# Three new tables for a fixed program: order, engines of copies, and buffers

## The chip, the core and the metric

One core of a Trainium2 chip runs the whole program. The time is device microseconds of one launch, the median of three runs. The core has five instruction queues that run side by side, each strictly in its own order: TensorE (PE, matrix products and transposes; its weight loads are listed as PEld), VectorE (DVE), ScalarE (ACT), GpSimd (POOL) and SyncE (SP, which only issues DMA transfers here). They wait for one another through semaphores.

## What is computed

Three layers follow each other on a batch of 2, with 768 rows each:

```python
# 1: attention, 8 heads of 64; q and k only meet in the same hash bucket of 6 bits
mask   = q_bucket[:, :, :, None] == k_bucket[:, :, None, :]
attn   = softmax(where(mask, q @ k.T / 8, -1e9))
x      = (attn @ v)                                  # (2, 768, 512)
# 2: four experts, each a causal attention of its own; two experts per row are weighted
for e in range(4):
    a    = softmax(causal(x @ wq[e] @ (x @ wk[e]).T / 8))
    out += gate_e * (a @ (x @ wv[e]) @ wo[e])
# 3: mix each row with the row before it, then a gated two-layer network
xk, xr = mu_k * x + (1 - mu_k) * x_prev, mu_r * x + (1 - mu_r) * x_prev
y      = sigmoid(xr @ w_r) * (relu(xk @ w_k) ** 2 @ w_v)
```

Precision is kept by splitting numbers into a high and a low half of 16 bits. Almost every tile so has a "hi" copy (a conversion) and a "lo" subtraction behind it, and every product is made of three.

## The kernel before

The rows are worked in 12 blocks of 128 (`i` = 0 to 11; blocks 0 to 5 are the first of the batch). For each block there are steps:

- `query_steps(i)`: load q, split it (`naq`), transpose it (`x2`), hash it (`z_q`), mark the buckets (`nbq`), transpose them (`x1`). `key_steps` does the same for the keys (`nak`, `nbk`, `y2`, `y1`) and splits the values.
- `lsh_steps(i)`: for each head `h`, PE makes the scores `s_i_h`; DVE scales them and takes the minimum (`P`); ACT takes the exponential; ACT or POOL makes the hi half of `PHL_i_h`; POOL always makes the lo half (TENSOR_TENSOR); a DMA transposes `PHL` into `PT_i_h`; PE multiplies that with the values into `x_i`. Heads 0 and 3 of the first four blocks are transposed by PE instead (`tp0`, `tp1`). At the end DVE divides (`x32`), PE transposes, and ACT and DVE split (`xT_i`).
- `moe_steps(i)`: `qk_i`, `vg_i` (values and gate), the experts' scores `se`, their softmax (`PHL_m...`), the product `y_i`, the output `o_i`.
- `mix_steps(i)`: `mk_i` and `mr_i`, the hidden layer `h_i`, the gate `r_i` with its sigmoid `e_i`, the last product `v_i`, and the store.

The weights are loaded and split on the way (`w32_...`, `raw_...`, `wd_...` into `WQK`, `WVG`, `WO`, `WK2`, `WR`, `WV2`).

None of this sets the order. `Program.add` only records operations. At the end `Program.arrange` unpacks three packed tables: `ORDER` is a permutation of the 2,498 recorded operations, and its restriction to one engine is that engine's queue; `ENGINES` says for each conversion copy whether ACT, DVE or POOL does it; `HOMES` says in which buffer of its pool each tile lives:

```python
for o, e in zip(self.ops, unpack(engines, np.uint8)):
    if e:
        o.move("PVAG"[e])
self.order = [self.ops[i] for i in unpack(table, np.uint16)]
```

Since `issue` emits everything from one line, every instruction has the line L225; they are told apart by tile names. Each DMA takes one of eight semaphores (`DMAHW0` to `DMAHW7`), in turn and in the order of the table, and is issued only when the transfer that had this semaphore before has landed. So at most eight are under way, and a late one holds the queue that issues its successor.

Of the kernel before, what the change touches and what calls it, by code (L numbers as in the profile page):

```python
# [982 lines left out]
"""

HOMES = """
c-lpjjdI&K5QBkT{!>j`MYVN0yYe|_=l$QXpgKvEnOLI5B^LPBfUcAS=rw|RaJqTcElCd^m<{?i7MKNt(IVT}rA57OgpL2!iSO`C3$z5Ez;DDW>;>B3KY@SAf587}ziB
^!U*!L=qf$X5JOy@Z45ZYQnjN%BN9l7SUhGAu5q~d^JM9f7*+d-Abv;#HeMYr6wZKHz-V98vI-?i1P#N9SSdCpTWEIg_Q|Wm11*4JUYC1AE7CTn1^2F|Mx6L2VB3Dj`s
*7*>m=2GOsgo^}Q?sBl(Hvzmq+SmNn_nCsmpiOSwdplcE{tw&_c!<Z!Z&QlMSEtOIkw1EmR3-w3`vfL=%aZ#oI>W53>U0lz7%3AYO%AC$-T?DlggMsANp>aahHPnlfSU
ohARCHp$6GsS&%p>KxQpYIih${aq0L_uac6{Smj((BNK}x&4Y^aST4BkXI^<``{BD?aH8DTONPLfDtZKZs!pqgBh*1vu`9n0pm6GwO9_G(<uwV7Rg1RIUU=JXJY$wAHr
r-<hHN$uf{*VU@G4N$kmPTblRYYCB#(pBmW3%Uc2FCpv2@rqfM*km8@I2VhH$u&DkefGNJYcr^t?G9cQ3fx^<u01yo_;BsoI0+689mZMkSM5(TEg{hT(dQ)(2k(#)PVz  # L990
bUWCv;`7e6E_U*FU$&jw0|Ls1N6xIQQ%`EiOrcegJj%$tZT-SlM-roRQ&ox7)9JoFvCq2*R$S}JaZ^oJN7Fo5P=xv;`e74FZIm5Y@2h{Rl}}B<D6!05)#0eVsN!vXNc&
B`bM>=VnKA+w94s!+M(`b}YCtH5Bco<P9!e5E=eUk6g_RJL(M?$@a6I&0J!{<d`6;NYzpsm}t13Vf7L<zSQ-M|ysUb|o5BA6Oot95SR9>p}d*Dh!JPAS%36LM+sh)3kw
#?snwLkXh9s2
"""
# [48 lines left out]
```

## Time and profile before

| what | us |
|---|---|
| median of three runs | 458.5 (457.54 to 459.17) |
| the profiled execution, its own time | 459.79 |
| its span, first to last instruction | 458.0 |
| PE busy in it | 417.8 |
| POOL, DVE, ACT busy in it | 354.7, 346.1, 333.1 |
| mean granted share of PE's clock | 0.988 |

The span is what the rows below divide up; 1.8 us of the profiled time lie around it. Busy time of an engine says nothing about whom the others wait for: that is read from stretches of the span and from waits.

### The profile page before, as it was taken

Reading aid. Unit: us, or ns where it says so; the run is one execution under the profiler, and the core shown is the slowest. Engines: PE = TensorE matmul, PEld = TensorE weight load, DVE = VectorE, ACT = ScalarE, POOL = GpSimd, SP = SyncE. Lnnn points to the kernel's source line nnn. Section 1 sums busy time; section 2 is a strip of 40 time slices with the busy share of each in tenths; the row PEclk is TensorE's granted clock in tenths of the full one; section 3 lists DMA queues with packets and bytes.
Section 4 is the critical chain, followed back from the end, with each engine's and each line's share of the span. In section 5 each row is a group of like instructions: output and inputs, shape, how many; then the busy total and the mean of one; then the engine's idle time right before and its main releaser. Section 6 shows DMA issues by size and latency. Waiting matters only on the chain.

```text
span 458.0 us, 15085 instructions
## 1 busy us (share of the span) xinstructions
PE 417.8 (91%) x6080; PEld 318.0 (69%) x6080; DVE 346.1 (76%) x908; ACT 333.1 (73%) x634; POOL 354.7 (77%) x359
## 2 busy tenths in 40 slices
PE   2847777899899999999999999999999999999996
PEld 2725565678776778686668868786668689856772
DVE  2899998999999889899677787875778674635232
ACT  3998989999899797588986647787746658453230
POOL 5899999899998869799998998978878946462010
PEclk9987999999999999999999999999999999999999
DMA  8989999999999998889999999999698793357101
GB/s 215 276 201 204 210 223 212 231 210 204 213 238 187 166 183 152 206 144 149 191 169 197 158 171 154 190 146 155 124 169 118 140 156 68 74 114 176 36 24 46
DMA packets 227157, 75.54 MB, mean 165 GB/s; under 512 B 218512, under 2 KB 222736, under 8 KB 227088
## 3 DMA queue, kind: packets, MB, share of 16 engines
q1 hardware_dynamic: 225584, 74.48, 86.5%
q8 instruction: 47, 0.77, 0.7%
q10 hardware_dynamic: 1504, 0.11, 0.2%
q14 instruction: 22, 0.18, 0.2%
HBM read 22.14 MB, written 3.15 MB: 55 GB/s over the span
## 4 chain that ended last, share of the span: by engine, by line
PE 56%; DMA 12%; POOL 12%; DVE 8%; issue 6%; ACT 5%; ACTq 0%; POOLq 0%; DVEq 0%
PE h L225 12%; PE v L225 10%; DMA PT<-PHL 9%; PE x L225 6%; PE r L225 6%; POOL PHL L225 6%; PE s L225 6%; PE qk L225 4%; PE se L225 3%; PE vg L225 3%; PE o L225 2%; PE y L225 2%; DVE P L225 2%; ACT P L225 2%; DMA pr<-in_proj_dram 1%
## 5 line engine op out<-in xcount | busy, mean ns | idle before, releaser
L225 POOL TENSOR_TENSOR PHL<-P,PHL 128x768 f16<-128x768 f32 x96 | 160.7, 1685 | 14.9 <-ACT PHL L225 12.2
L225 DVE TENSOR_SCALAR_CACHE_REDUCE P<-s 128x768 f32<-128x768 f32 x96 | 90.5, 951 | 13.0 <-PE s L225 4.5
L225 ACT ACTIVATE P<-P,mx 128x768 f32<-128x768 f32 x96 | 89.2, 930 | 14.4 <-DVE P L225 10.4
L225 PE MATMUL s<-y,x 128*128 128x384 f16 x384 | 77.6, 330 | 2.4 <-DVE P L225 1.9
L225 PE MATMUL h<-mk,WK 128*128 128x128 f16 x1152 | 73.0, 219 | 0.6 <-DVE g L225 0.6
L225 PE MATMUL x<-v,PT 128*128 128x64 f16 x1728 | 62.6, 193 | 9.2 <-DMA PT<-PHL 7.6
L225 PEld LDWEIGHTS <-WK 128*128 128x128 f16 x1152 | 67.1, 98 | 5.1 <-issue 1.0
L225 PEld LDWEIGHTS <-PT 128*128 128x128 f16 x1728 | 58.2, 98 | 16.9 <-DMA PT<-PHL 9.6
L225 PE MATMUL v<-WV,k2h 128*128 128x512 f16 x192 | 57.1, 379 | 0.0
L225 PEld LDWEIGHTS <-x 128*128 128x128 f16 x480 | 38.1, 98 | 23.1 <-issue 5.8
L225 ACT ACTIVATE PHL<-P 128x768 f16<-128x768 f32 x53 | 44.1, 839 | 10.4 <-DMA PT<-PHL 3.7
L225 POOL TENSOR_TENSOR PHL_m<-P_m,PHL_m 128x512 f16<-128x512 f32 (+2 forms) x24 | 33.9, 1418 | 10.6 <-ACT PHL_m L225 9.9
L225 POOL TENSOR_SCALAR PHL<-P 128x768 f16<-128x768 f32 x43 | 37.8, 880 | 5.1 <-DMA PT<-PHL 2.0
L225 PE MATMUL qk<-xT,WQK 128*128 128x128 f16 x576 | 37.7, 219 | 0.3 <-POOL WQK L225 0.3
L225 PE MATMUL v<-WV,k2l 128*128 128x512 f16 x96 | 36.4, 379 | 0.0
L225 PE MATMUL r<-WR,mr 128*128 128x512 f16 x144 | 35.7, 379 | 0.0
L225 PEld LDWEIGHTS <-WQK 128*128 128x128 f16 x576 | 33.5, 98 | 2.0 <-POOL WQK L225 0.5
L225 ACT ACT_TABLE_LOAD x20 | 25.7, 1283 | 11.8 <-PE r L225 8.0
L225 ACT ACTIVATE P_m<-P_m,bias_m 128x512 f32<-128x512 f32 (+2 forms) x24 | 19.7, 822 | 14.5 <-DVE P_m L225 13.9
L225 PEld LDWEIGHTS <-k2h 128*128 128x128 f16 x192 | 17.1, 98 | 15.9 <-issue 0.4
L225 POOL TENSOR_TENSOR mk<-m32k,mk 128x512 f16<-128x512 f32 x12 | 14.0, 1164 | 15.7 <-issue 15.4
L225 ACT ACTIVATE t<-h 128x512 f32<-128x512 f32 x24 | 14.2, 593 | 16.0 <-PE h L225 14.8
(168 smaller groups left out, 861.3 us busy)
## 6 DMA issues: line engine op xcount, KB each, us to landing
raw_k<-in_moe_w_k_dram SPq DMA_DIRECT2D x8, 512.0 KB, 5.7
raw_v<-in_moe_w_v_dram SPq DMA_DIRECT2D x8, 512.0 KB, 4.6
k<-in_k_dram SPq DMA_DIRECT2D x8, 384.0 KB, 4.1
q<-in_q_dram SPq DMA_DIRECT2D x12, 256.0 KB, 4.6
v<-in_v_dram SPq DMA_DIRECT2D x8, 384.0 KB, 5.3
out_dram<-e SPq DMA_DIRECT2D x12, 256.0 KB, 2.9
raw_r<-in_moe_w_r_dram SPq DMA_DIRECT2D x4, 512.0 KB, 5.5
PT<-PHL SPq DMA_TRANSPOSE x88, 4.6
```

What stands on the lines that cost most here:

```text
L225: getattr(getattr(self.nc, engine), method)(*[real(a) for a in args], **{k: real(a) for k, a in kw.items()})
```

## The change

The program, its operations and their number stay the same: PE keeps 6,057 matrix instructions and as many weight loads in the built program, SP its 140 transposing DMAs. All three tables are replaced. A line of each stands for the whole:

```diff
 ORDER = """
-c-jrr0|OXT7XZ+E?|T<-wr$(CZQHhO+qP|^=GAQ0P-D%k_I>9^9D-O-6xu;aC<hL*KtvD#C=Uu*p%_$x63_;sL2+mgrC=xwfih45N<&%jkPWIrHDHJU1~Fk6RD|JB8LB
+c-jrr0|OXT7XZ-v?z?)kZQHhO+qP}nwrv|VuV%A`8f#{??>j%@#DYpt6iPxnKxhvU0iX>OgL04s1hRq$h4N4wx<NFk02QGtWCw$6PzFjtTZjOqAv#orT#y5Xz)+|RWuY
...
 HOMES = """
...
 ENGINES = """
-c-pO%*%pH!3`EJy|NnEX#gwp_0C`ZBlksK&Qz{Hes=;rF>&<({dqubMQ}>OZ8lNRv37y_^Sf|!xGCOKwQj+5@kTsxZz^Lk5s1f5Og);L_1R4$mzZu==K==4i<(L&4wi3
+c-pO2ff9uv2#f9i|M^{(sV}DBMO|l#FmO=EaS6`{+Q9DlGIuMK8|AXLh=0v0R%hrdpv~14@NmQ?Z{LXa057s9IF12&Z;wfV8wwMpv9}&Zd-S}qJCTTgjp+k5x_(V(8ap
```

Of the conversion copies 194 change engine: 57 go from ACT to POOL and 57 from POOL to ACT, 42 from ACT to DVE and 38 from DVE to ACT. PE's first product of a hidden layer, the order of blocks and the kinds of work in each stretch stay where they were; within a stretch nearly every row moves. Three places show how.

The first is the start of ACT's queue, up to its first conversions; `pr` is the hash projection (in two halves), `consts` the matrix of ones that PE's transposes use, `ties`, `muk` and `mur` small tables. Before:

```order
L225 DMA pr_72<-in_proj_dram 64x6
L225 DMA muk<-in_moe_mu_k_dram 128x4x1
L225 DMA pr_72<-in_proj_dram 64x6
L225 DMA consts<-in_consts_dram 128x384
L225 ACT_TABLE_LOAD
L225 ACTIVATE nak_1_0_99<-k_0_1_0_76 128x12x64 [waits DMAHW1_49]
L225 ACTIVATE nbk_1_0_80<-k_0_1_0_76 128x12x64
L225 DMA ties<-in_ties_dram 128x16 [waits DMAHW0_49]
L225 DMA mur<-in_moe_mu_r_dram 128x4x1 [waits DMAHW2_49]
```

and the same stretch after:

```order
L225 DMA muk<-in_moe_mu_k_dram 128x4x1
L225 DMA pr_82<-in_proj_dram 64x6
L225 DMA mur<-in_moe_mu_r_dram 128x4x1
L225 DMA consts<-in_consts_dram 128x384
L225 DMA ties<-in_ties_dram 128x16 [waits DMAHW0_49]
L225 ACT_TABLE_LOAD
L225 ACTIVATE nak_1_0_92<-k_0_1_0_76 128x12x64 [waits DMAHW1_49]
L225 DMA pr_82<-in_proj_dram 64x6 [waits DMAHW2_49]
L225 ACTIVATE nak_1_1_105<-k_0_1_1_94 128x12x64 [waits DMAHW3_49]
```

`mur` has moved ahead of `consts`, one half of `pr` has moved behind the first conversion, and `ties`, which waits for the transfer before it on its semaphore (that of `pr` before, of `muk` now), stands ahead of the table load and of the first conversion instead of behind two of them.

The second is POOL's queue where block 3 of the first layer and block 1 of the experts are fed (`PHL_3_7` is head 7 of block 3; `PHL_m1_p0` and `p1` are the pairs of experts of block 1). Before:

```order
L225 TENSOR_TENSOR PHL_3_0_1873<-P_3_0_1673,PHL_3_0_1873 128x768
L225 TENSOR_SCALAR PHL_m1_p1_1917<-P_m1_p1_1781 128x512
L225 TENSOR_SCALAR gt_1_1813<-gt_1_1813 128x16
L225 TENSOR_TENSOR mk_0_1876<-m32k_0_1745,mk_0_1876 128x512
L225 TENSOR_TENSOR PHL_m1_p0_1971<-P_m1_p0_1762,PHL_m1_p0_1971 128x512
L225 TENSOR_TENSOR PHL_m1_p1_1917<-P_m1_p1_1781,PHL_m1_p1_1917 128x512
L225 TENSOR_SCALAR gs_1_1950<-gs_1_1950 128x1
L225 TENSOR_TENSOR PHL_3_6_2004<-P_3_6_1879,PHL_3_6_2004 128x768
L225 TENSOR_TENSOR PHL_3_4_1957<-P_3_4_1618,PHL_3_4_1957 128x768
L225 TENSOR_TENSOR PHL_3_7_2097<-P_3_7_1914,PHL_3_7_2097 128x768
```

and the same stretch after:

```order
L225 TENSOR_TENSOR PHL_3_0_1863<-P_3_0_1723,PHL_3_0_1863 128x768
L225 TENSOR_SCALAR mk_0_1948<-m32k_0_1769 128x512
L225 TENSOR_SCALAR gt_1_1866<-gt_1_1866 128x16
L225 TENSOR_TENSOR mk_0_1948<-m32k_0_1769,mk_0_1948 128x512
L225 TENSOR_TENSOR PHL_3_4_1935<-P_3_4_1606,PHL_3_4_1935 128x768
L225 TENSOR_TENSOR PHL_m1_p1_1987<-P_m1_p1_1742,PHL_m1_p1_1987 128x512
L225 TENSOR_SCALAR nbq_98<-q32_5_543 128x8x64
L225 TENSOR_SCALAR PHL_m1_p0_2093<-P_m1_p0_1870 128x512
L225 TENSOR_SCALAR raw_v23_0_2031<-raw_v23_0_2031 128x512
L225 TENSOR_TENSOR PHL_m1_p0_2093<-P_m1_p0_1870,PHL_m1_p0_2093 128x512
L225 TENSOR_TENSOR PHL_3_7_2037<-P_3_7_1868,PHL_3_7_2037 128x768
```

`PHL_m1_p0` has moved behind `PHL_3_4`, next to `PHL_3_7`, while `PHL_3_4` and `PHL_3_6` (two rows above this piece) stand ahead of the experts; `mk_0` has a POOL conversion that ACT made before, and `PHL_3_0` and `PHL_m1_p1` have lost theirs to ACT.

The third is DVE's queue around the transposed queries of block 6 (`x2_6`, which PE's hash product `z_q6` reads). Before:

```order
L225 TENSOR_TENSOR xT_4_3262<-tr_x_4_3246,xT_4_3262 128x512
L225 TENSOR_SCALAR P_5_7_3290,mx_5_2720<-s_5_7_3150 128x768
L225 TENSOR_SCALAR P_5_2_3297,mx_5_2720<-s_5_2_3264 128x768
L225 SCALAR_TENSOR_TENSOR h_1_0_3215<-h_1_0_3215,t_1_0_3320 128x512
L225 COPY x2_6_3299<-tr_x2_6_3292 128x512
L225 TENSOR_REDUCE vg_3_3163<-gt_3_3282 128x4
L225 TENSOR_TENSOR k2l_1_3348<-h_1_0_3215,k2h_1_3328 128x512
L225 SCALAR_TENSOR_TENSOR g_3_3375,gs_3_3376<-vg_3_3163,ge_3_3342 128x4
L225 SCALAR_TENSOR_TENSOR vn_0_1338<-vg_3_3163,vn_0_1338 128x256
L225 TENSOR_SCALAR P_5_6_3408,mx_5_2720<-s_5_6_3337 128x768
L225 TENSOR_SCALAR y_3_3379<-sme_3_3039,gs_3_3376 128x4
L225 TENSOR_SCALAR lg_4_3414,gm_4_3415<-vg_4_3395 128x4
```

and the same stretch after:

```order
L225 SCALAR_TENSOR_TENSOR m32r_2_3100<-o_2_2980,mur_84,x2t_2_3047 128x128
L225 COPY x2_6_3247<-tr_x2_6_3223 128x512
L225 TENSOR_SCALAR P_5_6_3310,mx_5_2911<-s_5_6_3288 128x768
L225 SCALAR_TENSOR_TENSOR h_1_0_3232<-h_1_0_3232,t_1_0_3308 128x512
L225 TENSOR_TENSOR k2l_1_3368<-h_1_0_3232,k2h_1_3337 128x512
L225 TENSOR_TENSOR z_q6_3339<-z_q6_3339,zl_q6_3365 128x8x6
L225 TENSOR_SCALAR y_3_3312<-sme_3_3027,gs_3_3283 128x4
L225 TENSOR_SCALAR P_5_7_3373,mx_5_2911<-s_5_7_3348 128x768
L225 RECIPROCAL y_3_3312<-y_3_3312 128x4
L225 TENSOR_TENSOR xT_4_3395<-tr_x_4_3376,xT_4_3395 128x512
```

Before, DVE copies one half of `x2_6` and ACT the other. Now DVE copies both (the first one stands seven rows above this piece), and `xT_4` has moved from ahead of `P_5_7` and `k2l_1` to behind them. The two copies of `x1_7`, the transposed bucket marks of block 7 that its scores `s_7` read, go from ACT to DVE as well; the later one stands in row 394 of DVE's queue of instructions, counted from 0, where `e_2` stood before (row 390 was `x32_6`).

## Rows read from the trace of the kernel before

**Rows 1.** The page: span, then busy time, share, instructions by engine.
```profile
span 458.0 us, 15085 instructions
PE 417.8 (91%) x6080; PEld 318.0 (69%) x6080; DVE 346.1 (76%) x908; ACT 333.1 (73%) x634; POOL 354.7 (77%) x359
```

**Rows 2.** Stretches: start:end, length, busy us (instructions) by engine, PEclk, DMA share, GB/s.
```profile
0.00:120.00 120.00, 88.32 (x1326) 68.87 (x1327) 104.78 (x260) 104.74 (x206) 108.67 (x114) 0.96 1.03 218
120.00:440.00 320.00, 315.57 (x4630) 240.40 (x4629) 237.28 (x644) 225.28 (x424) 245.99 (x246) 1.00 0.86 153
20.00:120.00 100.00, 78.28 (x1176) 59.78 (x1175) 94.21 (x237) 92.34 (x188) 95.11 (x94) 0.95 1.04 210
100.00:140.00 40.00, 38.23 (x632) 31.57 (x631) 38.53 (x102) 38.24 (x77) 38.17 (x39) 1.00 1.19 215
0.00:111.30 111.30, 80.93 (x1200) 63.08 (x1201) 96.73 (x241) 97.35 (x191) 100.42 (x107) 0.95 1.01 217
164.00:232.00 68.00, 66.51 (x1058) 51.87 (x1057) 58.47 (x142) 55.38 (x102) 59.31 (x59) 1.00 0.92 170
```

**Rows 3.** Waits of PE to 125 us: on what, total us, times, longest.
```profile
PE tr_y L225 <- DMA consts<-in_consts_dram: 9.0, 1, 9.0
PE x L225 <- DMA PT<-PHL: 6.6, 5, 2.5
PE tr_x L225 <- DVE nbq L225: 5.0, 2, 4.8
```

**Rows 4.** Waits of PE from 125 us on, same columns.
```profile
PE x L225 <- DMA PT<-PHL: 1.1, 1, 1.1
PE z_q L225 <- DVE e L225: 1.0, 1, 1.0
```

**Rows 5.** ACT, first 5 us: start, took, instruction; then landing times by issue; then queues.
```profile
1.32 0.59 ACTq L225 DMA_DIRECT2D muk<-in_moe_mu_k_dram  x1
3.14 1.28 ACT L225 ACT_TABLE_LOAD   x1 [3.14 <-issue]
4.43 0.84 ACT L225 ACTIVATE nak<-k 128x768 f16<-128x768 f32 x1
muk<-in_moe_mu_k_dram ACTq DMA_DIRECT2D x1, 2.0 KB, 5.6
consts<-in_consts_dram ACTq DMA_DIRECT2D x1, 96.0 KB, 6.4
mur<-in_moe_mu_r_dram ACTq DMA_DIRECT2D x1, 2.0 KB, 4.6
q10 hardware_dynamic: 1504, 0.11, 0.2%
```

**Rows 6.** Chain of waits, 90 to 125 us: start, length, what. PE back to back.
```profile
95.41 1.34 PE vg L225 x12
97.47 0.65 PE s L225 x4
```

**Rows 7.** Timeline of PE and POOL around 118 us.
```profile
108.06 3.27 POOL L225 TENSOR_TENSOR PHL<-P,PHL 128x768 f16<-128x768 f32 x2
118.18 0.70 PE L225 MATMUL x<-v,PT 128*128 128x64 f16 x18 [1.31 <-DMA PT<-PHL]
```

**Rows 8.** Groups of one kind: count, busy us, mean ns of one, idle before.
```profile
L225 POOL TENSOR_TENSOR PHL<-P,PHL 128x768 f16<-128x768 f32 x96 | 160.7, 1685 | 14.9 <-ACT PHL L225 12.2
L225 POOL TENSOR_SCALAR raw_v<-raw_v 128x512 f32<-128x512 f32 x8 | 5.3, 671 | 0.1
```

**Rows 9.** Timeline of DVE and PE, near 164 and near 222 to 232 us.
```profile
163.18 0.42 DVE L225 COPY x<-tr_x 128x512 f16<-128x512 f16 x1
164.28 0.35 PE L225 MATMUL z_q<-prhl,x 128*128 128x12 f16 x8
221.65 0.81 PE L225 MATMUL s<-y,x 128*128 128x384 f16 x4
231.52 0.68 DVE L225 TENSOR_TENSOR x<-x,rs 128x512 f32<-128x512 f32 x1
```

More of the change, by code (lines that the diff above doesn't have):

```diff
@@ new lines @@
+7J8QoCpFjmzR%Kpi&_euf=T+}(9Ua4BSURop%I*8S(MxLR%yWb#9C7-shO-3izU@7#0uz@3D;t|OFlKU_b^<{G+FP}^m9%b`CGhT(YC)pN^W1?+<N?lg3Q>RjJ_c7S8y
+g=^$qx<C8~{N1gD(KrS>!$a4=oq<Pg6<l*8v8rqAM&TE?8rQ%Y{NTpHWB1Cvc8t5B3tV@<xyi5x*1}%+%dLiu>hPl*4>w#Bw-5eyO&#JoXy)eNez@swxdYI`t%pVQrx(
+obpSZ8?sZ+cJx7`M~<G#6;&M>Qg=9{}#ZZ3Lk?V{nouB}^(8=;N+<RW1^m&2chowy6Hz&hLn-`zay<t{_OKioeqBKCGyA)6nIeO(_H1+T$4T#xhdJe-3AxEl{*KiA&<0
+)t#9M>y17hw&I47vLi7;0C)J@GDHi$T-YRzzZ<Mb#W6Qi;sXgeSg>04RBF$mh0vw;seO#hr5Z;*)7D5ZaQwli!cRlLJZ99ySqs^1xL8NzK6@>W8y166({2!eBl>kEbQr
@@ new lines @@
+C`+UBD{|#RHf$ky1#;LFu3;N$-3667dF%CY0@$ME(gOM)3pWx!*W_%1AaFkn$%kVaA!O`vsjCEt&L>C{oVj^td@4zHC*(Jb+zL4LKGw?1<f_-=owqZMe9H+R1m>AppL%
+1AQ;48QfGu%}76lUTqJdD%abaw=2x|LYi&vx7KBxc9OZWZRhB-p_x$G;#2&c-<|7jDF#@fddWui+0kg-hI0H_y#?U40Rs9+To+x5)kFi~2@BC3f=}@Nb_Rb7CfJ?koBo
+_{MkgnelH(g+Jk2e-z*O#{Lbwh3CGrZ{aiIJ1FKCxYT$8(_l%z(0%mpeI87PY4J}ujZJ(hU)ry7pZo{^44y+J-`$_VZ*Uetd-xY{4p+P4ex+OC%J`R%7fbjxZV6?<@6g
+o$g86VU{R3;=I#=EQ3%}xemlb>Z%D#$Eht2$dP{Wt?Rs9b*j~DPNg1d;9@w4ye%lRvK3FElJ_y=CYLfFUOz?Qze|KhJ>5iE$=Fh9m~1+b?76Knanu9yGnpJP#s?{4A)y
@@ new lines @@
+oI;%4&KE;%Um(6;QRXoE}{D!ox6t*aVagQ;@HZsphT{kFM-SG8P@hC@tgNl&)4_mv9+(`R}xWM-^RbdGPsKB`qFqGmpi7!R2Em$8d^&c$h%Vb2z&dNSPqlWI@&-RX+1?
+HbV-Ta0MG6>tbpRW_&5}olF?(_;5NEVZnKL=HSj%r_kF#(ia5~M#LD;zh5q&1-4<tVkpIvB<6q-oKg2)5kMI;D(g)b#l#I5zZLSIimz;+BVLm>6f=E;yKSM37gd_cMzt
+in<yWKnd0()F4`r*IA2>%{y;|JX9_PNyb7DxHWwBNnKsBQ<1@nikpSQR6<(LMpCAfUf6qKih++((Q;j$%_Jcfd8W==2G9QbLOCV$c#F#eK%5J|$(Qnf?oY!+$Uht@2+n
+EoGqSE+(a;)gEb<kKwXXOt;3za?AW$Kikjo|6y$R9rw{emx&I!!!8>+t--M<J^hP6a6bjV+^_K7kMl>Ic<}T6M8D2g!(FtS=K4f5-cR<E`~fn*iKh6YZi1icGtwT)LfL
@@ new lines @@
+77U+C-L3EE6`xE43SmA)>cKS_15K01Gjrg_wPe!AaF>aS2etj&vjO>T%+X_MdR8(}@ZO-=DM9ic5$pBrNnoZ%brW`BpyP!4K_&9Mb8_6O+@<)pjR61VtV)STD*4Zaa?(
+uTa%7p5Xql$vq}&PT;)o6ke{XuID^_vtJhrmE7IoA3_bjJMHFpO;EdZtBPdsS{tO^Hhj_qZXW>j?yh^g(c|$6{iB!id%APY=hV6I+dc*bc4vR=Q7lpyYn$>i;t-XZ>L{
+qw{M4g{T{!|x5p0H5r3r`vRRjLCp=C+(a%J>f%p4;zAJa*1O5q>qc+@{kND&M9CgOS{w5vt8~Flt!M41dyCVBT{vutXt=f*e;X^v=SMUk{l&a8AzCBlyZCswZV-M_!Kl
+`e*ovTp=>V@aI3s<L=yoIYvS?bBXxHtFXid2*O@I+qA{dp^&^p$8G*PutVn%8gyzlwjSi2juC%Y%3b*QW;b2i26?GK?Ei9U07<c?UP5ojiqyaxK}#yLk`q<Gs9zhjSz!
@@ new lines @@
+#qa0JbdV46Q9i(teO(#A$G8?v<$+vJYEyk_AmjJ~|4A*Vq1@w(Jc*xCQ+iI5xd~0<I@H*rhPo8hpW()ImM`&f{)K<yU%4f<qG*0PU*>vrm|xR<e!xHT3tGT4IJ&>WNB9
+-Jp@rO>PVfjG$)k8YzoQubBR%9rJd0maOh22OQEQsXSNR;D<Wqc||DqfGmgaCGAIrz~f75R~fj?71|AoHNH+oMA{3n{r^Y{bB_rG%-KcD0J?{t$B`!>{;npis;&GGzV{
++E*YYy2O1e!@xpV{T7N_#aB<8%Yx}CSJ<SO=S#6;amJC-{!#4LUJF0g~xJ4KIZRo3g1}%;FNx{bfP<)LRg#0GoB)kxSyQnj+DxaHkTh1iKhy1RGuc$So!~9vFcFiF9T$
+tMCPE;8TlzcXVWo~+7FWmn#RB24m4I`aAz7WFZmUBk{;59rpq8n>(lvh@;Arizj%f;v#vBkMoMgMAuT0(Nbg%oXXzqwIUe_?p7Mq-`Zh9Hx=KIlOWo-`ccW1fi(AVj-%
@@ new lines @@
+YwpTj@!0xDUPNw|v=O@ewsXC*U6Rk@IOUiKOrN3y+rx(p&n-H~!B5a9>Ht(KWw*;H&<uPsAzp6MyB;JXd09WKGO5wHKZ7QFMsRmZ&;Wj=6vNv~MS=be>F-a~|ZTZ!iC`
+6O{8ln$8k01+;@?*Mj=1|Ha?%g|ws0m!wQ`!C&)RbdChM?o;wMP0lkVwWiS|oK}-@1j(ThC9)*e(Q?ag*GRHMcj->O=QC&$z3(6RC=yjta9q9PQ!z_nz3uOMkp;3_)9^
+xBB&j(g|KNxIH=j|XNgT<kizS!-?jQLqoQWTM6_e-^Pt$8mNyjlHw`S%iJ}t+Rq#9TD=uetSOXvWKrLlFXq~~<HL{>;1&8&O%XN|AT?Tnt#78Xb2NfwPQSv9`2w6mH_T
+iH2HuIKfT7S{yY)Rsw6O{fWEr6iOTx?EaY2ER&9>UB+|H*}3;(>9h!e$mx(Sl7xrDXIH3iR{<MdP<+@dg)EcB&j5pjgnkaN(R{^Mf8GhkO}lux67}3KriYM{X-|x4#_N
@@ L999 @@
-9W4xS^el*<M@AXt{Dcq%YlrD3|;p+_V206KFpK>d;
+c-pO2ff9uv2#f9i|M^{(sV}DBMO|l#FmO=EaS6`{+Q9DlGIuMK8|AXLh=0v0R%hrdpv~14@NmQ?Z{LXa057s9IF12&Z;wfV8wwMpv9}&Zd-S}qJCTTgjp+k5x_(V(8ap
+^ND%*=~%J*K&9Lv<avji5~s{$0f)`p5}BU-3fZNlkmGruWX^!Q`Ul?k7M&X+?xf)hRKKsltOBx=b(vXS8?XQ>*oY{kJjDwkqdW!#eF*#z8qP(7Cmn~VUZ(r2pw#E2>pv
+#W#!|CtOh@@;*`x}w3v_0VQG-Iw9-<E#HU;VQYzbTiQ=cWChg->U(W
 """
```

76 lines of the change are left out of this document (25 added, 51 removed).

## The prediction, made before the changed kernel ran

> **What bounds the kernel now.** I read the page first: TensorE is busy 417.8 of a span of 458.0 us [rows 1], so it is idle for 40.2. The stretches say where: in the first 120 us it is busy 88.3, idle 31.7; from 120 to 440 it is busy 315.6 of 320, idle 4.4 [rows 2]; the last 18 us hold the remaining 4.1, with the last product, sum and store. From 120 us on the kernel is TensorE's own work, and an order can win there only the 4.4. Whatever is to be won is won in the front, or lost anywhere.
>
> The front is bound by all three of the other engines at once: from 20 to 120 us POOL, DVE and ACT are busy 95.1, 94.2 and 92.3 of 100 [rows 2]. TensorE eats ahead of them and then waits. Its waits by releaser, up to 125 us: 9.0 for `consts` at the very start, 6.6 for the transposed `PT` (five waits, the longest 2.5), 5.0 for `nbq` [rows 3]. Behind 125 us only small ones are left: one `PT` of 1.1 and `z_q` for 1.0 [rows 4].
>
> The longest-lasting of these decides: the `x_3` product of head 7, at 118.18, which had waited 1.31 for its DMA, and whose POOL instructions started at 108.06 and ran 3.27 as a pair, so ended at 111.33 [rows 7]. From POOL's end to TensorE's start lie 6.9 us of issue, transfer and landing. Up to 111.3 us POOL had been idle 10.9 [rows 2]. So POOL's queue ahead of `PHL_3_7`, its idle time and the landing time set when TensorE leaves the front.
>
> **The change, part by part.** The totals of each engine stay nearly equal (57 conversions each way between ACT and POOL, 42 against 38 between ACT and DVE), so I cost nothing for the exchanges as such; their cover is that the sums are the same, and without it each POOL conversion costs about 0.7 [rows 8]. I look at where in the queues the rows stand. All sums are on the profiled span of 458.0 and carried to the median, 458.5 (the profiled execution took 459.79, 1.8 around its span).
>
> *Start.* Before, `consts` lets TensorE begin at 9.0 [rows 3]. `muk` was issued at 1.32 and landed 5.6 later, at 6.9; ACT's table load (1.28) and first `nak` (0.84) ran meanwhile, done by 5.3 [rows 5]. Now `muk` is first, a position of 0.6 earlier, and lands at about 6.3; `ties`, which waits for it, stands ahead of the table load. ACT is blocked until 6.3, then issues (0.59), loads (1.28), converts (0.84): 9.0. The low half on DVE comes behind it, about another conversion of 0.8. TensorE's first transposes so start at 9.0 to 9.8; I take +0.8, since the low halves are needed in the same first run of transposes. Behind the blocked ACT stand its next conversions, for which POOL and DVE wait; they have copies of their own that hang on loads, not on ACT. Ends: 0, and +4.6 if `consts`, with `mur` now ahead of it, comes later by the whole landing time of `mur` (4.6) [rows 5].
>
> At this place a rule speaks against the change. The row: the queue that carries these small tables has 1,504 packets for 0.11 MB, and a 2 KB table takes 5.6 to land while the 96 KB of `consts` takes 6.4 [rows 5]. The Trainium skill, page "DMA: Bandwidth & Descriptors", section "Rules for kernel authors", says that a strided last dimension is turned into one descriptor for every element. `muk` and `mur` are loaded in that form, 512 elements each; by that rule the packet count agrees, and `consts` would stand behind 1,024 descriptors, not 512. By the row alone `consts` goes beside the small tables and not behind them (it landed 2.0 behind `muk`), and the sum has +0.8; by the rule it would have more, which is rival D.
>
> *Landings in the front.* For each `PT` I took TensorE's work ahead of its product and POOL's work ahead of its low half, each instruction at its duration; the difference is the room for POOL's idle time and the landing. For head 7 of block 3, the tightest before, TensorE now has a `vg` (1.34), an `s` (0.65) [rows 6] and an `x_3` of another head (0.5 to 0.7 [rows 7]) more ahead, less two transposes of about 0.35 each: +1.8. POOL has 107 rows ahead in place of 109; the difference of two conversions at 0.67 [rows 8] is 1.3, or 0.9 when the exchanged ones are each taken at their own size; I take 0.9. So head 7 gains 2.7. But other heads come next: head 1 of block 3, earlier 1.0 looser than head 7, moved 2.8 earlier in both queues and keeps its room. It is now the tightest, so the front gains 1.0, if POOL idles as long as before. That is what I take: −1.0. Ends: 0, if TensorE merely waits for something else in the front; −2.7, if head 1 comes with a smaller landing time. The gain is bounded by 6.6, all `PT` waits of the front.
>
> *DVE at `z_q6`.* Before, the copy of `x2_6` ends at 163.60 and the product starts at 164.28 [rows 9]: 0.7 to spare. Now DVE copies both halves, with as many instructions ahead, and TensorE has 2.3 us less work ahead of the product (scores of block 5 and one `r_1` moved behind). It would arrive 2.3 earlier and wait 1.6 at that pace; if DVE fills some of its 9.5 us of idle time from 164 on (58.5 busy of 68 [rows 2]) a little earlier, nothing. I take the middle, +0.8. In this place DVE's `m32r` and `P_5` rows are queued behind the copy and ACT's exponentials behind those.
>
> *Late waits.* The `PT` of 1.1 and the `z_q` of 1.0 [rows 4] have 4 and 20 us more room by the same reckoning of work ahead: −2.1. Ends: 0 (others take their place) and −4.4, all idle time from 120 to 440.
>
> *The tail.* The order of the last block's work is kept; 0.
>
> Sum: +0.8 −1.0 +0.8 −2.1 = −1.5, so 457.0. The ends of the terms that are not rivals of their own, put together as they would rarely all fall, give 454 to 459.5.
>
> **Rivals.** A, slower, at one place: DVE comes late to `s_7`. Both copies of `x1_7` are now on DVE, the second in its row 394. Before, DVE was at this point (row 390) at 231.52, while TensorE started the first `s_7` at 221.65 [rows 9]. TensorE now has 4.9 us more work ahead of the score concerned (products of `v_2`, `o_4`, `x_6`), so wants it at 226.5. At the old pace of DVE that is a wait of up to 5.5 once the copy and its semaphore are added: 458.5 + 0.8 + 0.8 + 5.5, less the 3.1 of the other gains, = 462.5. It decides if DVE fills less than half of its 9.5 us of idle time between 164 and 232 [rows 2]. For it: the idle time hangs on TensorE's products, which come no earlier. Against: from 100 to 140 us DVE filled 38.5 of 40 [rows 2], so it can go at 96% when work is there; at that share it would be in time. Chance 0.17.
>
> B, no change: the front is bound by the sum of the three engines' work (95, 94, 92 of 100 [rows 2]), the room is not used, and the waits that vanish are replaced by others of equal length. +0.8 at the start, −0.3 at the rest: 459.0. For it: equal totals; three engines above 92% have little left to move. Chance 0.23.
>
> C, a larger gain: waits of POOL and TensorE feed each other. POOL idles 4.9 us in 20 to 120 [rows 2]; if half of that goes (−2.5) together with the 4.4 of TensorE's idle time behind 120, less 0.5 lost at the start: 452. For it: nearly every landing of the front has 1 to 3 us more room, the later ones 4 to 8. Against: POOL's idle time must be caused by TensorE, and in the front it is also caused by loads. Chance 0.15.
>
> D, `consts` late: the tables of single elements are carried in front of it. It lands 2.0 to 4.6 later in place of the 0.8 (by the distance of `consts` from `muk` and by `mur`'s own landing [rows 5]), which shifts everything: 458.2 to 460.8, about 460. For it: the packets, and that 2 KB take nearly as long as 96 KB; against: `consts` landed only 6.4 after its issue with one such table ahead of it, less than 1 us longer than that table alone. This is what the rule of the Trainium skill's page "DMA: Bandwidth & Descriptors" would make of the start. Chance 0.05.
>
> **How the numbers follow.** The forecast has 0.40. Differences within 0.3% (457.1 to 459.9) are about what a measurement of this kernel cannot tell from no change. The forecast lies at that edge: of its 0.40 I put 0.22 on faster, 0.14 on same, 0.04 on slower. A gives 0.02 same and 0.15 slower; B 0.06, 0.13 and 0.04; C 0.15 faster; D 0.01 same and 0.04 slower. Together 0.43 faster, 0.30 same, 0.27 slower. The range must take in most of C and of A, since cases of both signs hold most of the chance: 451 to 464, with C's 452 and A's 462.5 inside and their own uncertainty of about 1 us. The likeliest case's own range stays 454 to 459.5.
>
> **What would show it.** Start: TensorE's first instruction at 9.0 to 9.8, waiting for `nak` and not for `consts`; if for `consts` at 11 or later, D. Front: TensorE's busy time in the first 120 us at 88 to 90, `PT` waits below 6.6 in sum, the last of them at head 1 of block 3. Then: a wait of `z_q6` for DVE's `x2_6` below 1.6. If `s_7` waits several us for `x1_7` near 226, A. From 120 to 440, 2 to 3 us of idle time are left in place of 4.4; if busy time there stays at 315 to 316, the late waits were replaced and B holds. The prediction is wrong by more than its own range if DVE, and not POOL with its landings, paces TensorE between 120 and 240, or if POOL's idle time in the front moves by more than 2 us either way, for the whole room rests on its staying as it was.

## The result and the profile after

The changed kernel is slower: 464.56 us, median of four runs (463.61 to 464.83), against 458.65 for the kernel before in the same comparison (four runs, 457.54 to 459.17). The ratio is 1.0128, with a 95% interval of 1.0104 to 1.0152. A second comparison gave 463.37 and 1.0101 (1.0069 to 1.0133). In that one and those below, single runs of the kernel before lie between 456 and 462 us, so the intervals below are 0.2 to 0.4% to either side.

The page of the changed kernel: its span, then busy time of the engines (compare [rows 1]).

```profile
span 463.0 us, 15093 instructions
PE 419.9 (91%) x6080; PEld 319.2 (69%) x6080; DVE 353.6 (76%) x912; ACT 330.5 (71%) x628; POOL 351.8 (76%) x359
```

The span is 5.0 longer. DVE is busy 7.5 us more, with four instructions more. That is the first odd thing: four copies like the one in [rows 9], 0.42 us each, would cost 1.7.

The stretches of the changed kernel (start:end, length, busy time by engine from PE and PEld to POOL, clock, DMA share, GB/s):

```profile
0.00:120.00 120.00, 88.32 (x1319) 69.33 (x1320) 106.55 (x257) 104.32 (x206) 106.41 (x113) 0.96 1.03 213
120.00:240.00 120.00, 113.57 (x1730) 87.66 (x1729) 106.63 (x266) 98.51 (x181) 103.44 (x102) 1.00 0.99 178
240.00:440.00 200.00, 199.00 (x2877) 150.93 (x2876) 135.88 (x384) 124.63 (x238) 139.96 (x144) 1.00 0.83 139
```

and the middle one in the kernel before, which its rows above do not show apart:

```profile
120.00:240.00 120.00, 117.45 (x1780) 90.03 (x1779) 105.24 (x268) 102.11 (x191) 107.10 (x104) 1.00 1.01 181
```

In the first 120 us TensorE is busy 88.32 in both kernels [rows 2], so its idle time in the front is the same. The new idle time lies in the middle. From 120 to 240 us TensorE is idle 6.4 us, against 2.6 before, and ACT and POOL are busy 3.6 and 3.7 less, while DVE is busy 1.4 more. Nobody but DVE is busy longer, and everybody else waits.

Idle time is not the whole loss. Over the span it rises by 2.9 us: 3.9 more from 120 to 240 us, 0.9 less from 240 to 440, 0.1 less behind. The other 2.1 of the 5.0 us are busy time, 419.9 against 417.8 for the same 6,080 instructions (the number in both traces), and equal busy time in the front is not equal work. Between 80 and 100 us the granted clock is 1.00 before and 0.91 in the changed kernel (same columns, before first):

```profile
80.00:100.00 20.00, 17.78 (x275) 14.34 (x276) 18.88 (x58) 18.99 (x42) 18.21 (x22) 1.00 1.03 231
80.00:100.00 20.00, 16.63 (x252) 13.42 (x252) 16.27 (x50) 16.79 (x35) 16.00 (x17) 0.91 1.11 197
```

TensorE's rows in the changed kernel (start, length, what, the wait ahead of it in brackets):

```profile
86.41 0.35 PE L225 MATMUL y<-vn,PT_m_p 128*128 128x64 f16 x6 [1.53 <-DMA PT_m_p<-PHL_m_p]
87.47 0.35 PE L225 MATMUL y<-vn,PT_m_p 128*128 128x64 f16 x6 [0.71 <-DMA PT_m_p<-PHL_m_p]
...
88.45 1.49 PE L225 MATMUL s<-y,x 128*128 128x384 f16 x4
```

TensorE waited 1.53 and 0.71 us for the transposed pairs of experts, and a little later four score products take 1.49 us that take 0.81 elsewhere [rows 9]. That is the lower of its two clock levels, 1.2 GHz in place of 2.4. It lasts some 3 us there, so by an estimate from these rows some 1.5 us are lost that no list of waits shows. The second profile of the changed kernel (experiment 4) has 0.91 in this stretch as well. So has that of five of q in experiment 7. Those of experiments 1 and 8, of the control of the changed kernel in 6 and of q's 12 in 7 have 1.00, and 1 and 8 take as long as the changed kernel in experiment 4 (463.23 and 463.33 against 463.37). How much of the difference of the medians hangs on this stays open.

TensorE's waits in the changed kernel, up to 125 us and behind (releaser, total, times, longest; compare [rows 3, 4]):

```profile
PE tr_y L225 <- DMA consts<-in_consts_dram: 9.5, 1, 9.5
PE s L225 <- DVE P L225: 5.2, 6, 1.4
PE tr_x L225 <- DVE z_q L225: 3.6, 1, 3.6
PE s L225 <- DVE x L225: 3.5, 1, 3.5
PE y L225 <- DMA PT_m_p<-PHL_m_p: 2.2, 2, 1.5
...
PE x L225 <- DMA PT<-PHL: 0.5, 1, 0.5
...
PE x L225 <- DMA PT<-PHL: 2.0, 2, 1.6
PE tr_y L225 <- ACT y L225: 0.9, 1, 0.9
PE o L225 <- DVE yT L225: 0.8, 2, 0.4
PE y L225 <- DVE g L225: 0.8, 1, 0.8
PE se L225 <- DVE P_m L225: 0.6, 1, 0.6
```

The waits for `PT` in the front, 6.6 before, are down to 0.5. In their place stand waits for DVE, some 17 us in all where there were some 11 before, and the two for the transposed pairs of experts (2.2 us), of which the kernel before shows none. The room for the landings of `PT` is there; what it was cleared for has been taken by something else.

**Where DVE's time went.** Groups of DVE instructions: the low halves of the loaded q, k and v (`naq`, `nak`, `v`). Count, busy time in us, mean ns of one, idle time before. First the kernel before:

```profile
L225 DVE SCALAR_TENSOR_TENSOR v<-v,v 128x768 f16<-128x768 f32 x8 | 11.1, 1384 | 0.0
L225 DVE SCALAR_TENSOR_TENSOR naq<-q,naq 128x512 f16<-128x512 f32 x12 | 10.1, 844 | 1.3 <-POOL naq L225 1.3
L225 DVE SCALAR_TENSOR_TENSOR nak<-k,nak 128x768 f16<-128x768 f32 x8 | 9.7, 1207 | 7.8 <-ACT nak L225 5.7 <-POOL nak L225 1.9
```

then the changed one:

```profile
L225 DVE SCALAR_TENSOR_TENSOR naq<-q,naq 128x512 f16<-128x512 f32 x12 | 15.2, 1266 | 0.0
L225 DVE SCALAR_TENSOR_TENSOR v<-v,v 128x768 f16<-128x768 f32 x8 | 11.7, 1466 | 0.0
L225 DVE SCALAR_TENSOR_TENSOR nak<-k,nak 128x768 f16<-128x768 f32 x8 | 9.6, 1206 | 7.6 <-ACT nak L225 7.6
```

The same 12 instructions on the same shapes cost 5.1 us more for q. In the changed kernel one of them takes 0.68 us at its shortest and 2.19 at its longest. Eight of the 12 take 0.68 or 0.69 us before, three now. In the second profile of the changed kernel q's 12 take 13.7 us and the eight of v 13.3: the split among the groups varies, the sum of the three (36.4 there, 36.5 here) does not. The timelines around 216 to 228 us of the changed kernel show what happens to one; DVE first (start, length, what):

```profile
216.18 2.35 DVE L225 SCALAR_TENSOR_TENSOR v<-v,v 128x768 f16<-128x768 f32 x1
...
223.02 1.63 DVE L225 SCALAR_TENSOR_TENSOR naq<-q,naq 128x512 f16<-128x512 f32 x1
224.57 0.41 DVE L225 TENSOR_TENSOR yT<-tr_y,yT 128x256 f16<-128x256 f32 x1
224.91 0.94 DVE L225 TENSOR_SCALAR_CACHE_REDUCE P_m<-se 128x768 f32<-128x768 f32 x1
```

POOL in the same stretch:

```profile
214.47 3.25 POOL L225 TENSOR_TENSOR PHL<-P,PHL 128x768 f16<-128x768 f32 x2 [0.28 <-POOL PHL L225]
217.68 0.93 POOL L225 TENSOR_TENSOR gt<-lg 128x16 f32<-128x16 f32 x1
218.69 0.22 POOL L225 TENSOR_TENSOR gt<-gt,ties 128x16 f32<-128x16 f32 x1
...
222.46 1.65 POOL L225 TENSOR_TENSOR PHL<-P,PHL 128x768 f16<-128x768 f32 x1
224.19 0.51 POOL L225 TENSOR_SCALAR gs<-gs 128x1 f32<-128x1 f32 x1
```

DVE's `v` begins at 216.18, when the second of two POOL subtractions is running, which ends at 217.72. It is through at 218.53, 0.8 us after that end: its own time is 0.95, so it did next to nothing until POOL was done. POOL's next instruction, a tiny one (its mean in the kernel before is 0.22), begins at 217.68 and ends at 218.61, right behind DVE's. The same at 223.02: `naq` waits for the POOL instruction that ends at 224.11, ends at 224.65 itself, and POOL's `gs` is held until then. So whichever started first holds the other off until it is through. Behind this `naq` stand the low half of `yT_4` and `P_m5`, and TensorE, in the same stretch of the changed kernel, waits for exactly these:

```profile
225.04 0.44 PE L225 MATMUL o<-yT,WO 128*128 128x128 f16 x5 [0.43 <-DVE yT L225]
...
226.79 1.13 PE L225 MATMUL se<-kT,qT 64*128 64x384 f16 x11 [0.56 <-DVE P_m L225]
```

The Trainium skill, page "SBUF — State Buffer", section "SBUF: two separate sides", says that VectorE and GpSimd share one pair of SBUF ports, which is locked by one of them for a whole instruction. A VectorE instruction contends for it, among other cases, when it reads two operands from SBUF, and then only against a GpSimd instruction that reads SBUF. The traces agree. The low halves of the loaded tiles subtract one SBUF tile from another. Most of DVE's other subtractions here have one operand in PSUM, and the 0.69 us of `wd_v` and `WV`, which have one there too, do not change beside POOL. Eight more subtract SBUF from SBUF, `hl_x` and `hl_y` of late blocks, and they vary in the same way. In the changed kernel `hl_x` takes (shortest, median, longest in ns)

```profile
L225 DVE TENSOR_TENSOR hl_x<-x,hl_x x4: 687/692/2123, 296.4 to 384.2; 128x512 f16<-128x512 f32 x4
```

and the experiments below leave these eight as they are. An exception fits too: a POOL instruction that only writes is not held. In the kernel before, at 9 us, POOL's `memset` starts just behind DVE's `naq` and takes 0.62 us all the same, as do all eight of its kind (0.615 to 0.619). DVE and POOL:

```profile
9.02 0.69 DVE L225 SCALAR_TENSOR_TENSOR naq<-q,naq 128x512 f16<-128x512 f32 x1 [0.98 <-POOL naq L225]
```

```profile
9.04 0.62 POOL L225 MEMSET nbk<- 128x624 f16 x1
```

Taken at their shortest (0.68 for q, 0.945 for k and v), the 28 low halves would cost 12 x 0.68 + 16 x 0.945 = 23.3 us. They cost 30.9 before and 36.5 in the changed kernel: 7.6 and 13.2 us too long.

### The profile page after: what moved, and what is told of

Read it like the earlier page. It is cut to its first block, busy times and chain, and to the rows that moved or that the text cites. A ratio compares the mean times of both kernels' runs of the same rounds, so it can differ in the third digit from the quotient of the medians.

```text
span 463.0 us, 15093 instructions
## 1 busy us (share of the span) xinstructions
PE 419.9 (91%) x6080; PEld 319.2 (69%) x6080; DVE 353.6 (76%) x912; ACT 330.5 (71%) x628; POOL 351.8 (76%) x359
## 4 chain that ended last, share of the span: by engine, by line
PE 44%; POOL 3%; DVE 3%; DMA 2%; issue 2%; ACT 0%; DVEq 0%; POOLq 0%; ACTq 0%
PE v L225 11%; PE h L225 8%; PE r L225 5%; PE s L225 5%; PE x L225 4%; PE qk L225 3%; PE y L225 2%; DMA PT<-PHL 2%; POOL PHL L225 2%; PE o L225 2%; PE se L225 2%; PE vg L225 1%; DVE v L225 1%; POOL mk L225 0%; DVE P_m L225 0%
## 5 line engine op out<-in xcount | busy, mean ns | idle before, releaser
L225 PE MATMUL s<-y,x 128*128 128x384 f16 x384 | 80.7, 337 | 10.0 <-DVE P L225 5.2
L225 PE MATMUL h<-mk,WK 128*128 128x128 f16 x1152 | 74.1, 220 | 0.6 <-DVE g L225 0.3
L225 ACT ACTIVATE PHL<-P 128x768 f16<-128x768 f32 x56 | 46.5, 838 | 6.8 <-DMA PT<-PHL 3.5
L225 POOL TENSOR_SCALAR PHL<-P 128x768 f16<-128x768 f32 x40 | 34.6, 867 | 3.7 <-ACT P L225 2.0
L225 PE MATMUL v<-WV,k2l 128*128 128x512 f16 x96 | 36.4, 379 | 0.0
L225 DVE SCALAR_TENSOR_TENSOR h<-h,t 128x512 f32<-128x512 f32 x24 | 16.7, 696 | 20.0 <-ACT t L225 20.0
```

Source lines behind the costliest of these rows:

```text
L225: getattr(getattr(self.nc, engine), method)(*[real(a) for a in args], **{k: real(a) for k, a in kw.items()})
```

## The experiments

Two theories stood against each other. **L**: a late load and the queue of transposing DMAs around 140 us cost the time. **P**: the hold-off between DVE and POOL does.

**1. A late conversion (L).** In the changed kernel POOL stands still ahead of `raw_v26_0`, the last piece of the weights of the last product; this is one of its two longest single waits between 120 and 240 us, the other (4.3) being for DVE (POOL's timeline):

```profile
146.56 0.64 POOL L225 TENSOR_SCALAR raw_v<-raw_v 128x512 f32<-128x512 f32 x1 [3.34 <-DMA raw_v<-in_moe_w_v_dram]
```

The edit moves this row behind four others in POOL's queue:

```diff
-TENSOR_SCALAR raw_v26_0
 TENSOR_TENSOR PHL_4_1
 TENSOR_SCALAR PHL_4_4
 TENSOR_TENSOR PHL_4_4
 TENSOR_TENSOR PHL_4_7
+TENSOR_SCALAR raw_v26_0
```

> The changed kernel, with one POOL row moved: the conversion of raw_v26_0 (last piece of the weights w_v) goes from ahead of four PHL_4 rows (4_1 lo, 4_4 hi and lo, 4_7 lo) to behind them. Theory T (POOL stands still 3.3 us at 143.2 us for the landing of this load, and the four rows behind it feed PT_4_x, yT_2 and the block after them): POOL's wait is gone, TensorE's waits of 1.6 at 147.8 and the small ones up to 166 us go with it, some 3 us, so 461.0 to 462.0. Rival R (the three engines' work sets the pace in this stretch and the wait only shows it): TensorE loses the same 3 us between 140 and 172 us by other waits, 464 to 465.

Measured: 463.23 us, ratio to the kernel before 1.0095 (1.0061 to 1.0128). POOL's wait is gone, the time hardly moves: the ratio lies inside the interval of the second comparison of the changed kernel (1.0101, experiment 4), and the time lies between the two forecasts.

**2. The same wait put into the kernel before (L).** SyncE's load of `raw_v26_0` moves behind `PT_4_2`, POOL's conversion of it up by two rows:

```diff
 DMA_TRANSPOSE PT_m2_p0
-DMA raw_v26_0
 DMA raw_v25_0
 DMA_TRANSPOSE PT_4_2
+DMA raw_v26_0
 DMA_TRANSPOSE PT_4_3
```

> The kernel before, with the suspected wait put in: SyncE's issue of the load of raw_v26_0 goes behind the transposing DMA of PT_4_2, as in the changed kernel, and POOL's conversion of it goes up to right behind that of raw_v25_0, ahead of two short rows. POOL's work between the end of PHL_4_2 lo, which releases the load, and the conversion is 5.6 us; issue and landing took 8.7 in the changed kernel. Theory T: POOL waits about 3 us for the load, TensorE loses 2 to 3, 460.5 to 461.5. Rival R: the rows behind have room enough, 458 to 459.

Measured: 460.13, ratio 1.0017 (0.9995 to 1.0039). POOL now waits 2.1 us for this load, and TensorE's idle time from 120 to 240 us is 2.4, as without it (2.6). The time lies between the two forecasts and cannot be told from that of the kernel before; the idle time speaks for the rival, that the rows behind have room enough.

**3. Halves of the tables.** Two kernels join the tables at the 1000th operation: the first by one kernel's order, the rest in the order of the other.

```python
head  = order_of_one[:1000]
order = head + [k for k in order_of_other if k not in head]
```

> The first 1000 of the 2,498 operations in the order, engines and buffers of the kernel before (TensorE is then at about 162 us), the rest in those of the changed kernel, buffers reassigned where they collide. Time minus TensorE's back-to-back work at this point is 46.6 us before and 50.2 after; from there to the end 7.1 more before and 8.5 after. Theory T (most was lost up to there, in the front and at the load): 458.6 + 1.4 = 460.0. Rival (the new tables lose evenly, or their later part, DVE's copies of x1_7 above all, is the slow one): 461.5 to 464.

> The other way round: the first 1000 operations by the tables of the changed kernel, the rest by those of the kernel before. Theory T: 458.6 + 3.6 = 462.2, the loss up to 162 us kept. Rival (the later part is the slow one): 459 to 460.5.

Measured: 479.33 (1.0436) and 475.50 (1.0353). Both are far slower than either kernel, so they cannot locate anything. At the seam the queues of two orders meet, and 187 and 147 tiles had to be given another buffer. Which of the two cost the 17 to 21 us was not taken apart. What follows is only that one cannot cut such tables in the middle.

**4. The changed kernel again.**

> The changed kernel as it is, beside the next three on the same chip. 464.0 to 465.0 if the loss belongs to its tables; TensorE's idle time again about 31.7 in the first 120 us and 6.4 from 120 to 240 us. If the waits of one execution are chance, the waits at 147.8 (transposed block 4_6), 225 to 228 and 165 are not found again at these places.

Measured: 463.37, ratio 1.0101 (1.0069 to 1.0133), a little under the forecast. TensorE is idle 30.8 us in the first 120 and 6.1 from 120 to 240. The waits near 147.8, 165 and 225 to 227 stand within 0.2 us of their places, and DVE and POOL hold each other off at mostly the same instructions. The waits belong to the tables and are no accident of one execution.

**5. One operand in place of two (P).** In both kernels the 28 low halves become a scaled copy with an accumulator, an instruction that reads one SBUF operand and takes as long (and is followed by a read of the accumulator of 0.08 us):

```diff
-nc.vector.scalar_tensor_tensor(na[:, :, D:], q32, SQ, na[:, :, :D], op0=OP.mult, op1=OP.subtract)
+nc.vector.tensor_scalar(na[:, :, D:], q32, SQ, None, op0=OP.mult, op1=OP.min, accum_out=dum)
...
-            lo_part("v", na[:, :, :, :D], k32, kh, SK)
+            nc.vector.tensor_scalar(na[:, :, :, :D], k32, SK, None, op0=OP.mult, op1=OP.min, accum_out=dum)
...
-            lo_part("v", vl, v32, vh, SV)
+            nc.vector.tensor_scalar(vl, v32, SV, None, op0=OP.mult, op1=OP.min, accum_out=dum)
```

> The changed kernel, in which DVE's low halves of the loaded q, k and v (28 instructions that read two SBUF operands) read one: the low half becomes a scaled copy with an accumulator, so the subtraction is left out and the numbers are not those of the reference. In the profile of the changed kernel these instructions took 13.1 us more than at their shortest, in that of before 7.5, always where a POOL instruction ran beside them. Theory P (these stretches, and POOL's equal ones, are on the path): both kernels gain, the changed one more, so 459 to 461.5 here against 456.5 to 457.5 for the kernel before without them; the difference between the two falls from 5.9 to 3 or less. Rival L (the loads and the queue of transposing DMAs around 140 us alone): 463.5 to 465 here and no change there.

> The same 28 instructions with one SBUF operand in the kernel before (subtraction left out as well). Theory P: 456.5 to 457.5. Rival L: 458 to 459.

Measured: 453.60, ratio 0.989 (0.986 to 0.9921), for the changed kernel; 452.90, ratio 0.9866 (0.9831 to 0.9901), for the kernel before. Both gain more than theory P had asked for, and of a difference of 1.0 to 1.3% between them 0.24% is left. In the changed kernel with one operand q's group reads

```profile
L226 DVE TENSOR_SCALAR_CACHE_REDUCE naq<-q 128x512 f16<-128x512 f32 x12 | 8.1, 672 | 0.2 <-DMA q<-in_q_dram 0.2
```

and the middle stretch

```profile
120.00:240.00 120.00, 117.87 (x1805) 91.28 (x1802) 103.94 (x290) 100.38 (x184) 103.34 (x103) 1.00 1.08 185
```

The 12 take their shortest time, beside POOL or not, and TensorE is idle 2.1 us in the middle where it was 6.4. POOL still waits 2.6 us for the late load (3.3 in the changed kernel).

**6. The control.** A low half with one operand no longer waits for the high half either. So the same instructions get two SBUF operands again, both of them the loaded tile:

```diff
-nc.vector.scalar_tensor_tensor(na[:, :, D:], q32, SQ, na[:, :, :D], op0=OP.mult, op1=OP.subtract)
+nc.vector.scalar_tensor_tensor(na[:, :, D:], q32, SQ, q32, op0=OP.mult, op1=OP.subtract)
```

> Control to the run with one operand: the changed kernel, in which the same 28 instructions of DVE read two SBUF operands again, but both are the loaded tile itself (the high half is left out, so no instruction waits for it, and the numbers are not the reference's). Theory P (DVE and POOL hold each other off when a DVE instruction reads two SBUF operands): 462.5 to 464.5, as the changed kernel. Rival W (the gain came from the wait for the high half that went with it): 453 to 456.

> The kernel before, the 28 low halves of q, k and v with the loaded tile as both SBUF operands (high half left out, no wait for it), the counterpart of the control run of the changed kernel (461.8). Theory P: 457 to 458.5, a difference of 3.5 to 5 between the kernels, as with the waits for the high half. Rival W (those waits set the kernels apart): the difference falls to 1 or less, 460.5 to 462 here.

Measured: 461.84, ratio 1.0067 (1.0036 to 1.0097), for the changed kernel; 457.29, ratio 0.9974 (0.9953 to 0.9994), for the kernel before. So the second operand is worth some 8 of the 9.8 us in the changed kernel (461.84 against 453.60) and 4.4 to 5 of the 5.9 in the kernel before (457.29 against 452.90; 1.1% by the ratios). The rest, some 1 to 1.5 us in each, went with the waits for the high half or lies within the intervals; in the changed kernel the stretch of low clock at 80 to 100 us is also missing from the control's profile. The time of the changed kernel's control lies just below theory P's range and far above rival W's. The difference between the kernels stays, 0.93%. In the changed kernel's control the instructions are long again:

```profile
L225 DVE SCALAR_TENSOR_TENSOR naq<-q 128x512 f16<-128x512 f32 x12 | 13.8, 1150 | 0.4 <-DMA q<-in_q_dram 0.4
```

and the idle time of TensorE in the middle stretch is 5.7 us:

```profile
120.00:240.00 120.00, 114.26 (x1733) 88.04 (x1733) 106.79 (x261) 98.57 (x181) 103.25 (x99) 1.00 0.99 180
```

**7. Only q, and only five of q.** The edit of 5 for q alone, in both kernels, and in the changed one for blocks 6 to 10 alone (`if 6 <= i <= 10`).

> The changed kernel with one operand in the 12 low halves of q alone (subtraction left out); those of k and v stay. Of the 13 us that DVE's low halves of q, k and v took too long, q has 7.0, and of the 7.5 before only 2.0: theory P, if cost follows this time, 9.8 x 7.0/13.1 = 5.2 less than the changed kernel, 458 to 459, at the time of before. Rival (the losses of k and v weigh as much each): 461 to 462.

> The kernel before with one SBUF operand in the 12 low halves of q (subtraction left out), the counterpart of the run that brought the changed kernel to 459.7. Theory P: before, these 12 took only 2.0 us too long on DVE (7.0 in the changed kernel), so the gain is small, 457.0 to 458.3, and the difference between the kernels falls to about 2. Rival: the 12 gain as much here (454 to 455.5); then q's low halves are not what sets the kernels apart.

> One operand in the low halves of q of blocks 6 to 10 alone, which run between 150 and 245 us (3.6 us too long on DVE there; subtraction left out). Theory P: the loss of TensorE between 120 and 240 us, 6.4 in the changed kernel against 2.6 before, falls to about 4; 460.5 to 461.5. Rival L (that loss comes from the load at 143 us and the transposing DMAs): 463 to 464, idle time there still 6.

Measured: the changed kernel with q's 12 changed takes 459.73, ratio 1.0019 (0.9999 to 1.0039); the kernel before with the same 458.34, ratio 0.9994 (0.9965 to 1.0023). So q's low halves alone bring the changed kernel to the time of before, where they bring the kernel before nothing that can be measured, and 0.25% is left between the two. A control with two SBUF operands was not run for q alone; but DVE was idle 0.0 us ahead of these 12 in the changed kernel (their group above), so no wait of DVE for the high half went with them there. Five of them give 462.14, ratio 1.0075 (1.0045 to 1.0104), a part of the way, between the forecasts of P and L. TensorE's idle time in the middle follows. First with all 12:

```profile
120.00:240.00 120.00, 117.01 (x1785) 90.31 (x1783) 106.28 (x274) 101.67 (x186) 104.68 (x103) 1.00 1.04 186
```

and with five:

```profile
120.00:240.00 120.00, 115.94 (x1762) 89.10 (x1759) 106.19 (x279) 101.16 (x187) 105.23 (x107) 1.00 1.02 182
```

3.0 and 4.1 us, against 6.4 and 6.1 in the two profiles of the changed kernel. The 4.1 is what theory P had said.

**8. The load in time (L).** A third buffer for raw weights lets SyncE issue the load of `raw_v26_0` ahead of the whole run of `PT_4`:

```diff
 DMA raw_v25_0
+DMA raw_v26_0
 DMA_TRANSPOSE PT_4_0
 DMA_TRANSPOSE PT_m2_p1
 DMA_TRANSPOSE PT_m2_p0
 DMA_TRANSPOSE PT_4_2
-DMA raw_v26_0
 DMA_TRANSPOSE PT_4_6
```

> The changed kernel with a third buffer for raw weights, used by raw_v26_0 alone: its load is issued in front of the transposing DMA of PT_4_0, some 10 us earlier, instead of between PT_4_2 and PT_4_6; to make room one buffer of the 2 KB kind is given up, 14 tiles change buffers and the load of q32_11 moves from 215 to about 224 us. Nothing else moves. Theory L: POOL's wait of 3.3 at 143.2 and TensorE's waits on PT_4_6 and PT_4_5 are gone, 460.5 to 462. Rival P: as in the run with the late conversion, 1.5 at most, 462 to 463.5.

Measured: 463.33, ratio 1.0108 (1.0067 to 1.0149): no gain. POOL converts at once, without a wait:

```profile
141.96 0.67 POOL L225 TENSOR_SCALAR raw_v<-raw_v 128x512 f32<-128x512 f32 x1
```

but TensorE has lost the same time a few products later, in this kernel at

```profile
150.69 0.70 PE L225 MATMUL x<-v,PT 128*128 128x64 f16 x18 [1.59 <-DMA PT<-PHL]
```

As far as the load goes theory L has fallen: with the load early, or its conversion late, the changed kernel stays where it was, and the kernel before bears the same wait at no cost that can be told. The queue of transposing DMAs was not changed by itself. TensorE's waits for `PT` between 120 and 240 us are 2.0 in the changed kernel and still 1.8 with one operand, where the idle time is down to 2.1, against 1.1 before: of the 3.9 us these waits themselves explain 0.9 at most.

## Why the prediction was wrong

I forecast 457.0 and a range of 451 to 464; the time of 464.56 lies just above the range (the second comparison's 463.37 just inside) and on the other side of the kernel before. Step by step:

- **Start: near in size, but not by its mechanism.** +0.8 forecast, +0.5 measured. TensorE starts at 9.5, still waiting for `consts`, which landed 7.0 us after its issue in place of 6.4; I had it wait for `nak`. ACT is blocked by `ties` as told, but `muk`, now first, landed sooner than the 6.3 that I took, and the first `nak` is done at 7.59. ACT's queue in the changed kernel:

```profile
5.07 0.35 ACTq L225 DMA_DIRECT2D ties<-in_ties_dram  x1
5.45 1.28 ACT L225 ACT_TABLE_LOAD   x1 [5.45 <-DMA muk<-in_moe_mu_k_dram]
6.75 0.84 ACT L225 ACTIVATE nak<-k 128x768 f16<-128x768 f32 x1
```

  Rival D, `consts` two or more us later behind the small tables, did not happen.
- **Landings in the front: the mechanism held, the gain did not.** `PT` waits fell from 6.6 to 0.5, but TensorE's busy time in the first 120 us is 88.32 in both, and some of it was at the lower clock. Waits for DVE (5.2, 3.6 and 3.5 in the list) and for the pairs of experts (2.2) stand where those for `PT` stood. That is what rival B said of the front. My sum had no term for the landings of the pairs, nor for the clock. With one operand TensorE is busy 90.4 in the front, with the control's two 89.4.
- **DVE at `z_q6`: no such wait is in the trace.** The +0.8 was nothing.
- **Late waits: this term failed.** I took −2.1 for `PT_4_2` and `z_q10`. Both waits are gone, but idle time from 120 to 440 rose from 4.4 to 7.4, since 3.9 came in between 120 and 240. I had looked only at work ahead of waits that the trace of before showed.
- **The step behind it: "I cost nothing for the exchanges as such; their cover is that the sums are the same."** This is the sentence that the runs refute. I gave each instruction a fixed duration. The 28 low halves on DVE do not have one: theirs depends on what POOL is doing when they start, and new tables draw new meetings. The term that I put at nothing measured 5.6 us on DVE (36.5 against 30.9), and taking it away from q's 12 alone takes the difference of the kernels from 1.0 to 1.3% to 0.25%. The rows for it were in the trace of before, `naq` between 0.68 and 1.70 us, and I read only its mean.
- **Rival A gave 462.5, near the measured time, but not for its reason.** No `s_7` waits for `x1_7`. A number that fits is no proof of the mechanism.
- **The condition named for failure was met in the main:** between 120 and 240 us DVE has the largest part of TensorE's waits, some 2.9 of 6.4 us against 1.4 of 2.6 before, and POOL's landings (`PT`) come second with 2.0. With one operand 0.3 us of waits for DVE is left. My sum had no term for it.

What is shown: q's 12 low halves make up most of the difference (1.0 to 1.3% as it is, 0.25% with one operand in them), and the control shows that it is their second SBUF operand that makes the low halves long. The remaining 0.25% is within what these runs can tell from nothing. What stays open: what the stretch of low clock adds in the median, and whether it follows from the hold-off; it is missing from the control's profile, in which the hold-off is there. Open, too, is whether a planner that knows of the hold-off could order the same program for the 452.9 us that the kernel before reaches without it. No kernel that keeps the subtraction and avoids the hold-off was tried, so none here beats both.

## What to carry to other kernels

An order drawn up from fixed durations can be right about every wait that it plans for and still lose, because where two engines meet decides how long some instructions take. Before trusting a sum over moved rows, look at the spread of each group's durations and not only at its mean: here the group whose longest member took 2.5 times its shortest (3.2 in the changed kernel) was waiting inside the instruction, which no list of waits shows. If DVE must subtract one SBUF tile from another while POOL reads SBUF too, count the rest of what POOL is doing as its price, and the DVE instruction as the price of POOL's next. And equal busy time of TensorE is equal work only at equal clock.

## What the runs showed that I had not expected

- Both kernels lose to the hold-off, and about as much as the two orders differ by: 5.9 us before and 9.8 in the changed kernel went with the second operand and the wait for the high half, 1.3 and 2.1% of the time, and by the controls 4.4 to 5 and some 8 of them with the second operand.
- It does not show as a wait. A held instruction counts as busy, so DVE's busy time rose to 353.6 us, and the idle time appeared on ACT, POOL and TensorE.
- SyncE's own issue of a transposing DMA is not short or constant. In the changed kernel two of them, behind a load of 512 KB, took 6.45 us together, where the median of the 140 is 1.48 (SyncE's timeline below). The load is not shown to be the cause: a pair behind another transposing DMA, `PT_m_p` at 131.10, took 6.96.

```profile
138.12 1.51 SPq L225 DMA_TRANSPOSE PT<-PHL  x1
139.80 0.78 SPq L225 DMA_DIRECT2D raw_v<-in_moe_w_v_dram  x1
140.68 6.45 SPq L225 DMA_TRANSPOSE PT<-PHL  x2
```
